# Nineteen differences per head for queries and keys: product halves of 304 columns instead of 320

## The chip, the cores and the metric

The kernel runs on one core of one Trainium2 chip. The metric is the device time of one launch in microseconds (us). A core has TensorE (PE, matrix products, with a queue of weight loads of its own, PEld), VectorE (DVE), ScalarE (ACT), GpSimd (POOL) and SyncE (SP), which here issues the DMA transfers. They run side by side and wait for one another through semaphores.

## The reference

There are 2048 rows of 640 values, 32 heads of 20 values, and two layers, each an attention step and a dense step (weights are the same in both layers):

```python
def _A_ref(x, wqkv, w_phi, wo):
    qkv = (x @ wqkv).reshape(B, S, 3, H, Dh) ...
    q, k, v = qkv[0], qkv[1], qkv[2]
    pq = einsum("bhsd,hdf->bhsf", q, w_phi)
    pk = einsum("bhsd,hdf->bhsf", k, w_phi)
    phi_q = concatenate([softmax(pq), softmax(-pq)], axis=-1)
    phi_k = concatenate([softmax(pk), softmax(-pk)], axis=-1)
    kv = einsum("bhsf,bhsd->bhfd", phi_k, v)
    z  = einsum("bhsf->bhf", phi_k)
    num = einsum("bhqf,bhfd->bhqd", phi_q, kv)
    den = einsum("bhqf,bhf->bhq", phi_q, z)[..., None] + 1e-6
    return (num / den) ... @ wo
def _B_ref(x, w1, b1, w2):
    h = x @ w1 + b1
    return (h * tanh(softplus(h))) @ w2
x = x + _A_ref(_layernorm(x), ...)
x = x + _B_ref(_layernorm(x), ...)
x = x + _A_ref(_layernorm(x), ...)
x = x + _B_ref(_layernorm(x), ...)
```

A softmax over the 20 values of a head does not change when the same number is subtracted from all of them. That holds for `pq`, `-pq`, `pk` and `-pk`.

## The kernel before

**Tiles.** The rows are worked on in 8 blocks of 256, each of two tiles of 128 rows. Every product is taken in three parts: a 32-bit value is split into a high part (`hi`, rounded to the format `fp32r`) and the rest (`lo`), and hi x hi, hi x lo and lo x hi are added up in PSUM. The inner dimension of 640 is 5 pieces of 128. One projection of a tile (`project`) is therefore two halves of 320 columns (`HC`), each 15 matmuls (`project_half`, L344), and a half fits one bank of PSUM.

**The first half of attention** (`attend_first`). For each tile there are a projection for keys, for queries and for values. `w_phi` has been folded into the query and key weights once, at the start of layer 0: `fold_phi` multiplies raw weights with a block-diagonal matrix of six heads (`bd`, L237) and splits the product into hi (ACT, L242) and lo (DVE, L243). The folded weights are written to `wp_d` in DRAM (`spill_qk_weights`) and fetched again for layer 1. Then `features` makes both softmaxes of a tile: ACT copies the 640 products from PSUM into every second group of 20 of the tile `e` (the `act` at L361; the profile shows ordered ACT instructions under L116, the line of the helper), DVE takes maximum and minimum per head (L368), subtracts (L371; L369 on DVE for keys, on POOL for queries), ACT takes the exponential of all 1280 values, DVE adds up each group and takes reciprocals (L377, L378), and POOL multiplies (L379). Keys then go into the sum with the values on PE (L414, 22 matmuls a tile). Queries are transposed in 32x32 pieces by DVE (L423) and written to DRAM (`e_d`), to be read again turned. The transposed, normalised rows of a block come in hi and lo (`Transposed.step`; the lo is L286 on DVE, tile `xtl`).

**The second half** (`attend_second`) multiplies the query features with the sums (L571), divides, projects with `wo` (again L344) and adds to the rows. **The dense layer** multiplies in L679 (256 columns) and L721 (320 columns), with the activation in between.

**Order.** The first half and the dense layer are under `tc.block(schedule_with_timeline_sim=True)`: a planner arranges the instructions of each engine by estimated durations. `attend_second` has PE and SP in the order in which it is written, and so has SP at the start. ACT instructions made with `act` are kept in program order relative to one another. `pending` and `advance` push the steps of older tiles on while a newer one is projected. The order of tiles in a block is a list:

```python
order = ("k0", "v0", "q0", "k1", "v1", "q1")
if b == 0:
    order = ("v0", "q0", "v1", "k0", "q1", "k1")
elif b == 1:
    order = ("k0", "q0", "k1", "v0", "q1", "v1")
elif b == NB - 1:
    order = ("k0", "k1", "v0", "v1", "q0")
```

Two PSUM tiles of two banks (`mm`) and four of one (`one`) are shared by all products.

Of the kernel before, what the change touches and what calls it, by code (L numbers as in the profile page):

```python
# [8 lines left out]
F32 = mybir.dt.float32  # L9
F32R = mybir.dt.float32r  # L10
AF = mybir.ActivationFunctionType
ALU = mybir.AluOpType
# [4 lines left out]
P = 128  # L17
S = 2048
D = 640
F = 1536  # L20
H = 32
# [6 lines left out]
NT = S // P  # L28
G = 11
HC = D // 2  # L30
EW = 2 * D
GW = 3 * (DH + 1)
GP = 6
# [9 lines left out]
def kernel(  # L43
# [131 lines left out]
    def load_q_weights():  # L175
        ws = [r2_pair(k) for k in range(KD)]
        for k in range(KD):
            for s in range(2):
                nc.sync.dma_start(ws[k][s].bitcast(F32), wp_d[0, s, k])
        return ws  # L180

    def load_k_weights(kv_ws):
        for k in range(KD):
            for s in range(2):
                nc.sync.dma_start(kv_ws[k][s][:, :D].bitcast(F32), wp_d[1, s, k])
# [26 lines left out]
    def load_raw(which, ts=range(6)):  # L212
# [11 lines left out]
            raw.append((r, rows))  # L224
        return raw

    def fold_phi(ws, bd, raw):

        pss = {}
        for k, c in ((0, 0), (1, 0), (2, 0), (3, 0), (0, 1), (1, 1), (2, 1), (3, 1), (4, 0), (4, 1)):  # L230
            if c == 0:
                mm = None if k % 2 else mm_tile()
                pss[k] = [one_tile(), one_tile()] if k % 2 else [mm[:, 0], mm[:, 1]]
            ps = pss[k][c]
            for t in range(3 * c, 3 * c + 3):
                r, rows = raw[t]
                nc.tensor.matmul(ps[:, (t % 3) * 120:(t % 3) * 120 + rows],  # L237
                                 r[:rows, k * P:(k + 1) * P], bd[:rows, t, :rows],
                                 start=True, stop=True)
# [86 lines left out]
        return Transposed(cols=cols)  # L326


    def project(xts, t, ws, col, ps=None):

        if ps is None:
            mm = mm_tile()
            ps = [mm[:, 0], mm[:, 1], mm]
        for c in range(2):
            project_half(ps[c], xts, t, ws, col, c)
        return ps

    def project_half(ps, xts, t, ws, col, c, ks=range(KD)):
        sl = slice(t * P, (t + 1) * P)
        cs = slice(col + c * HC, col + (c + 1) * HC)  # L340
        for k in ks:
            h, l, wh, wl = xts.hs[k], xts.ls[k], ws[k][0][:, cs], ws[k][1][:, cs]
            for n, (a, r) in enumerate(((h, wh), (h, wl), (l, wh))):
                nc.tensor.matmul(ps[:, :HC], a[:, sl], r, start=(k == 0 and n == 0),  # L344
                                 stop=(k == KD - 1 and n == 2))

    def both(ps):

        return ps[2][:, :, :HC]


    def query_tile(i):
# [2 lines left out]
    def features(ps, e, pool_sub):  # L355

        eg = e.rearrange("p (g d) -> p g d", d=DH)
        eh = e.rearrange("p (h s d) -> p s h d", s=2, d=DH)
        ec = e.rearrange("p (c h s d) -> p s c h d", c=2, s=2, d=DH)[:, 1]
        if len(ps) > 2:  # L360
            act(ec, both(ps).rearrange("p c (h d) -> p c h d", d=DH), AF.Copy)  # L361
        else:
            for c in range(2):
                act(ec[:, c], ps[c][:, :HC].rearrange("p (h d) -> p h d", d=DH), AF.Copy)
        yield
        m = work.tile([P, 2, H], F32, tag="m", name="m", bufs=2)
        for s, op in ((0, ALU.max), (1, ALU.min)):
# [19 lines left out]
    def attend_first(layer, x_src, first):  # L387
# [57 lines left out]
        if first is None:  # L445
            with tc.manual_schedule(engines={mybir.EngineType.SP}):
                bd = big_tile()[:120, :720].rearrange("p (t c) -> p t c", t=6)
                nc.sync.dma_start(bd[:, :3], phi_bd[:, :3])
                raw = load_raw(0, range(3))
                xt = fetch_normed(0)  # L450
                nc.sync.dma_start(bd[:, 3:], phi_bd[:, 3:])
# [49 lines left out]
        def rest():  # L501

            ps = [one_tile(), one_tile()]
            project_half(ps[0], xts, 1, q_ws, 0, 0)
            advance()
            advance()
            yield
            project_half(ps[1], xts, 1, q_ws, 0, 1, range(3))
            yield
            project_half(ps[1], xts, 1, q_ws, 0, 1, range(3, KD))  # L510
# [369 lines left out]
```

## Time and profile before

| | us |
|---|---|
| median of 3 runs | 1411.07 |
| lowest and highest | 1410.63 and 1412.09 |
| span of the profiled execution | 1410.6 |
| PE, PEld busy | 1391.5, 1369.5 |
| DVE, ACT, POOL busy | 1077.9, 583.6, 460.6 |

The profiled execution's own time is its span of 1410.6 us, from its first to its last instruction; the median of the runs is 0.5 us more. Busy shares are averages over stages. The first half of attention takes about 20 to 270 us in layer 0 and 718 to 968 us in layer 1, the dense layers follow the second halves. A matmul's busy time overlaps with the next one's, so the distance between starts is what a matmul costs. In groups by line, the columns are line, engine, operation, output<-input, shapes and count, then busy us and mean ns of one, then the idle time of the engine just before them with what ended it. In a timeline, the columns are start, duration, engine, line, operation, output<-input, shapes, count, and in brackets the idle time before. Rows of windows give, after the window, the busy time and count of each engine, the granted clock of PE, the DMA share and GB/s.

### The profile page before, as it was taken

To read this page: it belongs to the slowest core of one execution; us is meant where nothing else is said; L and a number is where in the kernel's file an instruction comes from. 1 tells how busy PE (TensorE), PEld (TensorE's weight loads), DVE (VectorE), ACT (ScalarE), POOL (GpSimd) and SP (SyncE) were. 2 spreads that over 40 slices of the span, in tenths; PEclk is the share of its full clock that TensorE was granted. 3 is DMA by queue.
4 is the path that set the end of the run, shared out by engine and by line. 5 is a ranking of instruction groups with operands and counts; after the bars stand their busy time and mean duration, and the time that the engine had idled before them with its cause. 6 is when DMAs were issued, how large, how long until landed. Compare 5 with 4: busy or idle time off the path is not lost. (4 is left out here: it accounts for less than half of the span.)

```text
span 1410.6 us, 28124 instructions
## 1 busy us (share of the span) xinstructions
PE 1391.5 (99%) x11528; PEld 1369.5 (97%) x11528; DVE 1077.9 (76%) x1810; ACT 583.6 (41%) x973; POOL 460.6 (33%) x344
## 2 busy tenths in 40 slices
PE   7999999999999999999999999999999999999998
PEld 7999999999999999999999999999999999999998
DVE  4798877686688877788769887878767766767765
ACT  4444343321355554455454333332234444444443
POOL 1354444343442221222234443443434211111112
PEclk9999999999999999999999999999999999999999
DMA  8533422789633423343374333357966212333200
GB/s 315 169 78 57 75 38 39 198 231 298 220 100 94 101 77 63 98 113 94 105 270 87 73 65 67 49 113 225 293 229 206 56 31 83 94 94 94 65 30 20
DMA packets 350035, 169.57 MB, mean 120 GB/s; under 512 B 286866, under 2 KB 323458, under 8 KB 349906
## 3 DMA queue, kind: packets, MB, share of 16 engines
q1 hardware_dynamic: 349906, 167.78, 44.1%
q8 instruction: 90, 1.47, 0.4%
q14 instruction: 39, 0.32, 0.1%
HBM read 104.82 MB, written 62.91 MB: 119 GB/s over the span
## 5 line engine op out<-in xcount | busy, mean ns | idle before, releaser
L721 PE MATMUL mm<-r2h,ol 128*128 128x320 f32 x1280 | 305.5, 310 | 1.4 <-ACT ol L704 0.8
L705 POOL TENSOR_TENSOR ol<-big,ol 128x512 fp32r<-128x512 f32 (+1 forms) x98 | 130.0, 1327 | 457.4 <-ACT ol L704 386.8
L679 PE MATMUL one<-xtl,r1h 128*128 128x256 f32 x960 | 268.6, 280 | 2.0 <-DVE xtl L286 2.0
L679 PE MATMUL one<-xth,r1l 128*128 128x256 f32 x960 | 268.0, 279 | 0.0
L679 PE MATMUL one<-xth,r1h 128*128 128x256 f32 x960 | 266.5, 279 | 0.0
L721 PEld LDWEIGHTS mm<-r2h,ol 128*128 128x128 f32 x1280 | 219.1, 188 | 3.1 <-POOL ol L705 1.8
L721 PE MATMUL mm<-r2l,ol 128*128 128x320 f32 x640 | 197.3, 309 | 0.0
L344 PE MATMUL mm<-r1h,xth 128*128 128x320 f32 x600 | 188.3, 314 | 0.0
L344 PE MATMUL mm<-r1h,xtl 128*128 128x320 f32 x600 | 185.7, 310 | 0.7 <-DVE xtl L286 0.7
L344 PE MATMUL mm<-r1l,xth 128*128 128x320 f32 x600 | 185.6, 309 | 0.0
L679 PEld LDWEIGHTS one<-xtl,r1h 128*128 128x128 f32 x960 | 180.4, 188 | 2.7 <-DVE xtl L286 2.5
L679 PEld LDWEIGHTS one<-xth,r1l 128*128 128x128 f32 x960 | 180.4, 188 | 0.0
L679 PEld LDWEIGHTS one<-xth,r1h 128*128 128x128 f32 x960 | 179.9, 188 | 0.0
L344 PE MATMUL mm<-r2h,xth 128*128 128x320 f32 x460 | 144.4, 314 | 0.0
L694 DVE TENSOR_SCALAR big<-big 128x512 f32<-128x512 f32 (+1 forms) x98 | 55.8, 570 | 113.4 <-ACT big L692 111.3
L344 PE MATMUL mm<-r2h,xtl 128*128 128x320 f32 x460 | 142.4, 310 | 0.0
L344 PE MATMUL mm<-r2l,xth 128*128 128x320 f32 x460 | 142.3, 309 | 0.0
L379 POOL TENSOR_TENSOR r<-r,r 128x1280 f32<-128x1280 f32 x32 | 75.7, 2367 | 144.5 <-DVE r L378 138.9
L692 ACT ACTIVATE big<-one,b1s 128x256 f32<-128x256 f32 x192 | 80.8, 469 | 96.0 <-PE one L679 93.8
L721 PEld LDWEIGHTS mm<-r2l,ol 128*128 128x128 f32 x640 | 120.2, 188 | 0.0
L696 ACT ACTIVATE big<-big,two 128x512 f32<-128x512 f32 (+1 forms) x98 | 70.1, 715 | 118.7 <-DVE big L695 116.2
L704 ACT ACTIVATE ol<-big 128x512 fp32r<-128x512 f32 (+1 forms) x98 | 61.0, 622 | 133.6 <-DVE big L703 133.3
(128 smaller groups left out, 3088.2 us busy)
## 6 DMA issues: line engine op xcount, KB each, us to landing
e_d<-r SPq DMA_DIRECT2D x128, 160.0 KB, 4.0
big<-e_d SPq DMA_DIRECT2D x32, 640.0 KB, 7.2
x_d<-xt SPq DMA_DIRECT2D x23, 640.0 KB, 4.1
xt<-x_d SPq DMA_DIRECT2D x22, 640.0 KB, 5.4
n_d<-xn SPq DMA_DIRECT2D x176, 80.0 KB, 2.1
xt<-in_x SPq DMA_DIRECT2D x16, 640.0 KB, 6.7
xn<-x_d SPq DMA_DIRECT2D x28, 320.0 KB, 4.3
v<-n_d SPq DMA_DIRECT2D x30, 256.0 KB, 3.1
```

The lines of the kernel that those rows point to most:

```text
L344: nc.tensor.matmul(ps[:, :HC], a[:, sl], r, start=(k == 0 and n == 0), stop=(k == KD - 1 and n == 2))
L379: nc.gpsimd.tensor_tensor(eg, eg, r.unsqueeze(2).to_broadcast([P, 2 * H, DH]), op=ALU.mult)
L679: nc.tensor.matmul(ph[:, j, :], l, r, start=(n == 0), stop=(n == 3 * KD - 1))
L692: exps[0] = nc.scalar.activation(part(ta, 0)[:, j - js.start], ph[:, j, :], AF.Exp, bias=b1s[:, 2 * pr + j:2 * pr + j + 1]).ins
L694: nc.vector.tensor_scalar_min(e, e, E_CAP)
L696: nc.scalar.activation(r, n, AF.Ln, bias=two)
L704: nc.scalar.activation(ah[:, js], n, AF.Copy)
L705: nc.gpsimd.tensor_tensor(al[:, js], n, ah[:, js].bitcast(F32), op=ALU.subtract)
L721: nc.tensor.matmul(pys[t][:, c, :HC], l[:, j, sl], r, start=(f == 0 and n == 0), stop=(f == KF - 1 and n == 2))
```

## The change

Per head, the first of the 20 product columns is subtracted from the other 19 in the block-diagonal matrix, before it is folded into the weights. So the folded weights of queries and keys have 19 columns a head, 608 in all, and the two halves of a projection have 304 columns. The twentieth value of a head, the first in its place, is the constant zero, written into the tile `e` by an additional ACT instruction. Everything from the maximum on works on 20 values as before. Values and output projection keep halves of 320.

```diff
+DF = DH - 1
+FC = H * DF // 2
+FW = H * DF
...
-    wp_d = dram.tile([2, 2, KD, P, D], F32, name="wp_d")
+    wp_d = dram.tile([2, 2, KD, P, FW], F32, name="wp_d")
...
-                nc.sync.dma_start(wp_d[1, s, k], kv_ws[k][s][:, :D].bitcast(F32))
-                nc.sync.dma_start(wp_d[0, s, k], q_ws[k][s].bitcast(F32))
+                nc.sync.dma_start(wp_d[1, s, k], kv_ws[k][s][:, :FW].bitcast(F32))
+                nc.sync.dma_start(wp_d[0, s, k], q_ws[k][s][:, :FW].bitcast(F32))
...
+    def differences(bd, ts):
+
+        part = bd[:, ts].rearrange("p t (h d) -> p (t h) d", d=DH)
+        nc.vector.tensor_tensor(part[:, :, 1:], part[:, :, 1:],
+                                part[:, :, :1].to_broadcast([120, 18, DF]), op=ALU.subtract)
...
-                nc.tensor.matmul(ps[:, (t % 3) * 120:(t % 3) * 120 + rows],
-                                 r[:rows, k * P:(k + 1) * P], bd[:rows, t, :rows],
+                n, c0 = rows // DH, (t % 3) * 6 * DF
+                nc.tensor.matmul(ps[:, c0:c0 + n * DF].rearrange("p (h d) -> p h d", d=DF),
+                                 r[:rows, k * P:(k + 1) * P],
+                                 bd[:rows, t].rearrange("p (h d) -> p h d", d=DH)[:, :n, 1:],
                                  start=True, stop=True)
-            n0, n1 = (0, 360) if c == 0 else (360, D)
+            n0, n1 = (0, 18 * DF) if c == 0 else (18 * DF, FW)
...
-    def project_half(ps, xts, t, ws, col, c, ks=range(KD)):
+    def project_half(ps, xts, t, ws, col, c, ks=range(KD), w=HC):
         sl = slice(t * P, (t + 1) * P)
-        cs = slice(col + c * HC, col + (c + 1) * HC)
+        cs = slice(col + c * w, col + (c + 1) * w)
...
-                nc.tensor.matmul(ps[:, :HC], a[:, sl], r, start=(k == 0 and n == 0),
+                nc.tensor.matmul(ps[:, :w], a[:, sl], r, start=(k == 0 and n == 0),
...
+        act(eh[:, 1, :, 0], ident[:, :H], AF.Copy, scale=0.0)
         if len(ps) > 2:
-            act(ec, both(ps).rearrange("p c (h d) -> p c h d", d=DH), AF.Copy)
+            act(ec[..., 1:], both(ps, FC).rearrange("p c (h d) -> p c h d", d=DF), AF.Copy)
         else:
             for c in range(2):
-                act(ec[:, c], ps[c][:, :HC].rearrange("p (h d) -> p h d", d=DH), AF.Copy)
+                act(ec[:, c, :, 1:], ps[c][:, :FC].rearrange("p (h d) -> p h d", d=DF), AF.Copy)
...
-            yield from features(project(xts, i % BT, kv_ws, 0), e, False)
+            yield from features(project(xts, i % BT, kv_ws, 0, w=FC), e, False)
...
-            yield from features(project(xts, i % BT, q_ws, 0) if ps is None else ps, e, True)
+            yield from features(project(xts, i % BT, q_ws, 0, w=FC) if ps is None else ps, e, True)
...
                 bd = big_tile()[:120, :720].rearrange("p (t c) -> p t c", t=6)
                 nc.sync.dma_start(bd[:, :3], phi_bd[:, :3])
                 raw = load_raw(0, range(3))
+                differences(bd, slice(0, 3))
                 xt = fetch_normed(0)
                 nc.sync.dma_start(bd[:, 3:], phi_bd[:, 3:])
                 raw += load_raw(0, range(3, 6))
+                differences(bd, slice(3, 6))
```

The loads of the weights in layer 1 and the four calls in `rest`, which projects the last query tile of each layer, change in the same way.

More of the change, by code (lines that the diff above doesn't have):

```diff
@@ L178, in load_q_weights @@
             for s in range(2):
-                nc.sync.dma_start(ws[k][s].bitcast(F32), wp_d[0, s, k])
+                nc.sync.dma_start(ws[k][s][:, :FW].bitcast(F32), wp_d[0, s, k])
         return ws
@@ L184, in load_k_weights @@
             for s in range(2):
-                nc.sync.dma_start(kv_ws[k][s][:, :D].bitcast(F32), wp_d[1, s, k])
+                nc.sync.dma_start(kv_ws[k][s][:, :FW].bitcast(F32), wp_d[1, s, k])
     def spill_qk_weights(kv_ws, q_ws):
@@ L326, in load_turned, with project @@
         return Transposed(cols=cols)
-    def project(xts, t, ws, col, ps=None):
+    def project(xts, t, ws, col, ps=None, w=HC):
         if ps is None:
@@ L343, in project_half, with both @@
             for n, (a, r) in enumerate(((h, wh), (h, wl), (l, wh))):
-                nc.tensor.matmul(ps[:, :HC], a[:, sl], r, start=(k == 0 and n == 0),
+                nc.tensor.matmul(ps[:, :w], a[:, sl], r, start=(k == 0 and n == 0),
                                  stop=(k == KD - 1 and n == 2))
-    def both(ps):
-        return ps[2][:, :, :HC]
+    def both(ps, w=HC):
+        return ps[2][:, :, :w]
     def query_tile(i):
@@ L503, in rest @@
             ps = [one_tile(), one_tile()]
-            project_half(ps[0], xts, 1, q_ws, 0, 0)
+            project_half(ps[0], xts, 1, q_ws, 0, 0, w=FC)
             advance()
@@ L507, in rest @@
             yield
-            project_half(ps[1], xts, 1, q_ws, 0, 1, range(3))
+            project_half(ps[1], xts, 1, q_ws, 0, 1, range(3), w=FC)
             yield
-            project_half(ps[1], xts, 1, q_ws, 0, 1, range(3, KD))
+            project_half(ps[1], xts, 1, q_ws, 0, 1, range(3, KD), w=FC)
             pending.append(queries(xts, NT - 1, ps))
```

2 lines of the change are left out of this document (1 added, 1 removed).

## The prediction

> **What bounds the kernel now.** The page comes first, for the engines' shares; then the waits of TensorE (PE), to see whether its busy time hides stalls; then the stages, since a share over the whole span mixes them. The lines of the page:
>
> ```profile
> span 1410.6 us, 28124 instructions
> PE 1391.5 (99%) x11528; PEld 1369.5 (97%) x11528; DVE 1077.9 (76%) x1810; ACT 583.6 (41%) x973; POOL 460.6 (33%) x344
> PEclk9999999999999999999999999999999999999999
> ```
>
> PE is busy 99% of the span at the full granted clock. What PE's waits show (us in total, times, longest):
>
> ```profile
> PE mm L237 <- DMA raw<-in_wqk_t: 8.3, 3, 4.2
> PE one L679 <- DVE xtl L286: 2.0, 2, 1.0
> PE one L414 <- POOL big L379: 0.9, 1, 0.9
> PE mm L344 <- DVE xtl L286: 0.7, 1, 0.7
> ```
>
> Over half of all waiting is the first 12 us, where weights have not landed. The attention's first half (queries, keys, values) is where the change acts; its windows give busy time per engine, PE, PEld (weight loads), DVE, ACT, POOL in turn:
>
> ```profile
> 60.00:101.00 41.00, 41.00 (x332) 39.77 (x331) 41.00 (x49) 19.14 (x27) 23.56 (x14) 1.00 0.39 71
> 101.00:245.00 144.00, 144.00 (x1102) 141.18 (x1102) 116.13 (x153) 57.44 (x81) 62.62 (x38) 1.00 0.34 57
> 735.00:792.00 57.00, 55.38 (x426) 54.03 (x425) 56.22 (x58) 24.34 (x38) 25.68 (x13) 1.00 0.41 80
> 792.00:945.00 153.00, 153.00 (x1163) 149.98 (x1162) 124.73 (x143) 54.67 (x78) 63.91 (x31) 1.00 0.39 71
> ```
>
> In the long steady stretches PE never stops and VectorE (DVE) fills 81% (116.13/144.00 and 124.73/153.00 are 0.81 and 0.82). At the start of each layer DVE is full as well (41.00 of 41.00; 56.22 of 57.00). So PE time saved in the steady part should come out of the total; near each layer's start, DVE may hold part of it.
>
> **The matmuls.** Busy time overlaps from one matmul to the next, so the price is the distance between starts. In the timeline, from one projection matmul to the 45th after it:
>
> ```profile
> 831.00 0.31 PE L344 MATMUL mm<-r1h,xth 128*128 128x320 f32 x1
> ...
> 837.60 0.31 PE L344 MATMUL mm<-r2h,xth 128*128 128x320 f32 x1
> ```
>
> 6.60 us / 45 = 146.7 ns for 320 columns. Whether fewer columns are faster is read from the dense layers, which have matmuls of 320 (L721) and 256 columns (L679) with the same 128x128 weight load; from the chain that ended last, and from the weight-load groups:
>
> ```profile
> 1131.95 3.50 PE one L679 x30
> 1135.45 3.53 PE mm L721 x24
> ...
> L679 PEld LDWEIGHTS one<-xth,r1l 128*128 128x128 f32 x960 | 180.4, 188 | 0.0
> L344 PEld LDWEIGHTS mm<-r1l,xth 128*128 128x128 f32 x600 | 112.8, 188 | 0.0
> ```
>
> 3.53/24 = 147.1 ns and 3.50/30 = 116.7 ns: 30.4 ns for 64 columns, 0.475 ns per column along this line, or 0.459 in plain proportion (147.1/320). The loads take 188 ns in both cases and are hidden in both, so the columns set the interval. 304 columns lie between the two measured sizes. 16 columns less are 7.34 to 7.6 ns; I take 7.35. The count is from the code: 16 tiles of rows, queries and keys, 2 halves x 15 matmuls, 2 layers: 16 x 2 x 30 x 2 = 1920. 1920 x 7.35 ns = **14.1 us saved** (bounds 14.1 to 14.6). Values and the output projection keep 320 columns.
>
> A rule stands beside that. The Trainium skill, "TensorE: Matmul & The Clock Gate", section Back-to-back issue gap, gives about N/2.4 + 2.5 ns for an isolated warm stream; by it 16 columns are 6.7 ns and the saving an estimated 12.8 us. The trace's 147 and 117 ns lie above that formula at both sizes, so the rows' slope is used.
>
> **The folded weights.** L237 multiplies 100 times with 120 columns and 20 times with 40; they become 114 and 38, read from a view of 19 of every 20. Six of them in a row:
>
> ```profile
> 36.34 0.82 PE L237 MATMUL mm<-big,raw 120*128 120x120 f32 x6
> 37.01 0.83 PE L237 MATMUL one<-big,raw 120*128 120x120 f32 x6
> ```
>
> (37.01 - 36.34)/6 = 112 ns, so 6 columns less are 5.6 ns, 0.56 us over 100. No row shows a read with gaps; I bound it by the same amount as a loss, and take 0.3 us saved, as part of them stand in stalls for their inputs. The evictions of the folded weights (342 and 266 columns, not 360 and 280) and the 40 transfers of them to and from DRAM shrink by 5%; no PE wait names them, so they count nothing.
>
> **The two subtractions.** They run on DVE over 120 x 342, and now the folds wait for them rather than for the transfer alone. The nearest rows in size:
>
> ```profile
> L584 DVE TENSOR_TENSOR xn<-mm,den 128x480 f32<-128x480 f32 x32 | 21.0, 657 | 1.0
> L584 DVE TENSOR_TENSOR xn<-mm,den 128x160 f32<-128x160 f32 x32 | 10.0, 313 | 0.0
> ```
>
> On that line 342 elements are 313 + 182 x 1.075 = 0.51 us. The first comes when the first block lands (4.2 us); PE's first four folds would start 0.5 later, still ahead of the 1.01 us pause for the next weights before 6.43, which takes it in. The second is less clear:
>
> ```profile
> big<-in_phi_bd SPq DMA_DIRECT2D x1, 168.8 KB, 7.5
> ...
> 3.05 0.44 SPq L451 DMA_DIRECT2D big<-in_phi_bd  x1
> ...
> 6.43 2.06 PE L237 MATMUL mm<-big,raw 120*128 120x120 f32 x8 [1.01 <-DMA raw<-in_wqk_t]
> 11.54 0.75 PE L237 MATMUL mm<-big,raw 120*128 120x120 f32 x2 [3.05 <-DMA raw<-in_wqk_t]
> ...
> 10.02 1.67 DVE L250 BATCH_NORM_STATS2 bn<-xt 128x6 f32<-128x320 f32 x4 [0.44 <-DMA xt<-in_x]
> 11.61 0.33 DVE L252 BATCH_NORM_AGGREGATE mv<-bn 128x2 f32<-128x12 f32 x2
> ```
>
> The second block lands at 3.05 + 7.5 = 10.55. Ahead of the statistics, the subtraction ends near 11.1 and PE does not notice, but the row statistics, the normalising and the transposes queued behind it on DVE come 0.5 later; behind them it ends near 11.94 + 0.51 = 12.45, and the folds, with ACT and DVE waiting for their results, start 0.9 later. Between 0 and 1.0 us I take **0.5 lost**.
>
> **The extra write and the copy.** 64 more ACT writes of 128x32, one ahead of each copy of products into the tile. The same kind of write exists for the values:
>
> ```profile
> L116 ACT ACTIVATE v<-ident 128x32 f32<-128x32 f32 x32 | 8.3, 261 | 0.0
> L116 ACT ACTIVATE big<-mm 128x640 f32<-128x640 f32 x32 | 22.6, 707 | 101.5 <-PE mm L344 101.5
> L116 ACT ACTIVATE r<-mm 128x640 f32<-128x640 f32 x30 | 21.2, 705 | 68.0 <-PE mm L344 58.8 <-DMA e_d<-r 9.2
> ```
>
> 64 x 0.261 = 16.7 us of ACT. But ACT sits idle 101.5/32 = 3.2 us and 68.0/30 = 2.3 us ahead of each copy, waiting for the products; the write needs only a free tile and goes there. The ordered list puts it right before the copy, which needs that same free tile (the 9.2 us on DMA), so nothing new is held up: 0 us. Without that cover every copy would be 0.26 late, 16.7 in all if PE felt each. The copy of 608 instead of 640 elements gains some 27 ns ((707 - 261)/608 x 32 = 23), off the path.
>
> **What DVE gives back.** DVE's work per tile is unchanged (the twentieth value is still reduced, exponentiated and scaled), so where DVE is full PE only arrives sooner. At the start of layer 1:
>
> ```profile
> 760.16 0.81 DVE L369 TENSOR_TENSOR big<-big,m 128x640 f32<-128x640 f32 x1
> ...
> 771.60 2.62 POOL L379 TENSOR_TENSOR big<-big,r 128x1280 f32<-128x1280 f32 x1 [5.84 <-DVE r L378]
> ...
> 771.92 2.98 DVE L369 TENSOR_TENSOR big<-big,m 128x640 f32<-128x640 f32 x1
> ...
> 775.97 2.84 DVE L286 TENSOR_TENSOR xtl<-xn,xth 128x512 fp32r<-128x512 f32 x1
> ...
> 781.58 1.04 DVE L286 TENSOR_TENSOR xtl<-xn,xth 128x256 fp32r<-128x256 f32 x1
> ...
> 782.67 0.42 PE L344 MATMUL mm<-r1h,xtl 128*128 128x320 f32 x1 [0.73 <-DVE xtl L286]
> ```
>
> Block 2's last transposed low half is ready only at 782.6. From 735, by the order of the code, 7 query and key tiles run before that: 7 x 30 x 7.35 ns = 1.5 us that PE saves and then waits for. In layer 0 the same piece is just in time:
>
> ```profile
> 91.12 0.36 DVE L286 TENSOR_TENSOR xtl<-one,xth 128x256 fp32r<-128x256 f32 x1
> ...
> 92.22 0.41 PE L344 MATMUL mm<-r1h,xtl 128*128 128x320 f32 x1
> ```
>
> Ready at 91.48, used at 92.22: 0.74 us to spare, against some 0.95 saved since 60 (4.3 query and key tiles of 30 matmuls in the order of the code): 0.2 lost. Together **1.7 lost**. Later, slack is ample; a key tile's last step on POOL against its use:
>
> ```profile
> 143.23 2.37 POOL L379 TENSOR_TENSOR big<-big,r 128x1280 f32<-128x1280 f32 x1 [5.29 <-DVE mv L252]
> ...
> 150.28 0.94 PE L414 MATMUL one<-big,v 128*64 128x120 f32 x14
> ```
>
> 145.6 to 150.28 is 4.7 us; a whole block gets only 120 x 7.35 ns = 0.88 us shorter.
>
> **Sum.** -14.1 - 0.3 + 0.5 + 1.7 = -12.2 us. On the profiled span, 1410.6 - 12.2 = 1398.4; the median of the runs is 1411.07, 0.5 above the span, so **1398.9 us**.
>
> **Rivals.** (1) DVE takes more. If DVE is what ends each block wherever it is full, and the order written anew by the planner from new durations costs a little besides, half the gain goes: 1411.1 - 7 = 1404, up to 1406. For it speak the full DVE windows; against it the 19% DVE slack over the 297 us of steady stretches. 10%.
>
> (2) The weight loads bound PE. PEld is busy 97% and every load stays, so nothing is gained: 1411.1 + 0.5 = 1411.6. Against it: the interval fell from 147 to 117 ns over loads of one length. 3%. The Trainium skill, "Perfetto Trace Analysis", section Identifying the Most-Contended Engine, takes the share of weight-load time as the measure of how near PE is to its limit, and would have these 97% as the bound; the two intervals disagree.
>
> (3) Slower: DVE and POOL collide. The L369 step of 2.98 us above ran beside POOL's multiplication (L379, 2.62 us); the same step at 760.16 took 0.81. That is 2.1 to 2.2 us for each collision; I take 2.1. A steady block has 24 of 29.4 us of DVE work (0.81 x 29.4, a block being 180 matmuls of 146.7 ns and 3 us of small ones). Shortened to 28.5 with a new order, it becomes DVE-bound from 28.5 - 24 = 4.5 us, two more collisions per block, and slower than before from 5.4. Three per block give 24 + 6.3 = 30.3, 0.9 us over 29.4; in the 10 steady blocks (297/29.4) that is 9 us: 1420. Against it: the order keeps its structure, and few collisions occur in the steady windows. 7%.
>
> (4) The new column count runs at the rate of the folds, 112/120 = 0.93 ns per column: 304 would be 284 ns, 137 more, 263 us in all, 1674. It decides as soon as an interval passes 146.7 ns. Nothing speaks for it but that no row has 304. 2%.
>
> **Numbers.** The forecast has 78%. Its own terms reach from -14.6 - 0.6 (1395.9; an order that happens to drop one of the small waits, 1394.5) to -14.1 + 0.6 + 1.0 + 4 (1402.6). Rival 1 extends the range to 1406; rivals 2, 3 and 4 stay outside, 12%. A difference under 0.2%, 2.8 us, is about what a measurement of this kernel cannot tell from none. Faster: 78 + 10 = 88%; same: 3%; slower: 7 + 2 = 9%.
>
> **What would show it.** Right: L344 groups of 1920 matmuls with 128x304, starts 139 to 140 ns apart; 64 writes of 128x32 near 0.26 us, with no PE wait on ACT; a steady block of 28.5 us; a longer wait on xtl (L286 before) near 780, 2 us rather than 0.7; the folds (L237) starting within 1 us of before. Wrong: intervals still at 147 ns (rival 2) or above (rival 4), DVE without idle time in the steady windows (rivals 1 and 3), or PE waits summing to over 20 us.

## The result and the profile after

The two kernels were run in turn on one chip, five times each. Before took 1412.09 us (median; 1410.63 to 1414.52), after 1405.88 us (1405.29 to 1406.86): the ratio is 0.9955, with a 95% interval from 0.9942 to 0.9967. That is 6.2 us faster, half of the 12.2 forecast. The profiled spans say the same: 1410.6 and 1404.1, 6.5 us apart. (The forecast started from 1411.07 for before, 1.0 below the median measured here, so it is the difference that is compared.) The page of the kernel after:

```profile
span 1404.1 us, 28174 instructions
PE 1381.4 (98%) x11528; PEld 1359.2 (97%) x11528; DVE 1077.1 (77%) x1812; ACT 591.1 (42%) x1037; POOL 466.4 (33%) x344
```

PE is 10.1 us less busy than before (1391.5), but the span shrank by 6.5 only. So PE waits more, which its waits show (us in total, times, longest):

```profile
PE mm L247 <- DMA raw<-in_wqk_t: 5.0, 2, 4.2
PE mm L355 <- ACT r L119: 5.0, 2, 2.7
PE mm L247 <- DVE big L233: 3.3, 1, 3.3
PE one L693 <- DVE xtl L297: 2.0, 2, 1.0
```

The folds (L247, before L237) wait 8.3 us in all, as before; 3.3 of them now go by the second subtraction. New is the second row: 5.0 us in two waits for a copy from PSUM by ACT (L119). Gone are the 0.9 us on POOL and the 0.7 us on `xtl` that the attention's first half had. The windows say where the new waits are (after each window: busy time of PE, PEld, DVE, ACT, POOL; granted clock, DMA share, GB/s):

```profile
60.00:101.00 41.00, 38.67 (x297) 37.33 (x297) 40.16 (x47) 16.33 (x26) 22.33 (x13) 0.96 0.40 74
101.00:245.00 144.00, 144.00 (x1142) 141.09 (x1141) 118.77 (x156) 61.42 (x102) 66.69 (x38) 1.00 0.33 56
735.00:792.00 57.00, 54.26 (x417) 52.68 (x416) 55.27 (x58) 23.02 (x42) 25.21 (x13) 0.97 0.43 84
792.00:945.00 153.00, 153.00 (x1192) 150.11 (x1191) 126.97 (x144) 59.83 (x102) 66.99 (x32) 1.00 0.41 76
```

In the two long stretches PE never stops and gets through 40 and 29 more instructions than before. In the two short ones at the start of each layer it does fewer (297 and 417, before 332 and 426), and its granted clock, 1.00 before, is 0.96 and 0.97. The steady price of the new matmul is read from the timeline (start, duration, engine, line, operation), 20 starts in a row, of which the first and the last:

```profile
103.26 0.30 PE L355 MATMUL mm<-r2h,xth 128*128 128x304 f32 x1
...
105.92 0.30 PE L355 MATMUL mm<-r2l,xth 128*128 128x304 f32 x1
```

2.66 us / 19 = 140.0 ns, where 320 columns take 146.7. The groups by line give the prices of the added instructions and of the shorter copies (busy us, mean ns, then the idle time before):

```profile
L233 DVE TENSOR_TENSOR big<-big 120x342 f32<-120x342 f32 x2 | 1.0, 510 | 2.4 <-DMA big<-in_phi_bd 2.4
L119 ACT ACTIVATE r<-ident 128x32 f32<-128x32 f32 x32 | 8.3, 260 | 28.6 <-DMA e_d<-r 19.8 <-DVE r L390 8.7
L119 ACT ACTIVATE r<-mm 128x608 f32<-128x608 f32 x30 | 20.3, 677 | 40.9 <-PE mm L355 40.9
```

The write of a query tile (`r<-ident`) now takes over the wait for the tile that the copy (`r<-mm`) had: ACT is idle 28.6 us ahead of it, and for 28.5 of these something still to finish with the tile is named. Before, 9.2 us stood there.

**The stall in layer 0.** PE's timeline around 89 us, after:

```profile
86.59 0.31 PE L355 MATMUL mm<-r1h,xtl 128*128 128x320 f32 x1
89.23 0.41 PE L355 MATMUL mm<-r1h,xth 128*128 128x304 f32 x1 [2.33 <-ACT r L119]
...
89.91 0.46 PE L355 MATMUL mm<-r1h,xth 128*128 128x304 f32 x1
...
92.44 0.46 PE L355 MATMUL mm<-r1l,xth 128*128 128x304 f32 x1
...
94.18 0.41 PE L355 MATMUL mm<-r1h,xth 128*128 128x320 f32 x1
```

PE could have gone on at 86.74 (one interval after 86.59) and starts at 89.23. From 89.91 to 92.44 ten intervals take 2.53 us, 253 ns each and not 140: the granted clock is 0.50 there (its rows stand in the last section). What PE waited for is on ACT, first after, then before:

```profile
88.38 0.26 ACT L119 ACTIVATE r<-ident 128x32 f32<-128x32 f32 x1 [9.56 <-DMA e_d<-r]
88.51 0.66 ACT L119 ACTIVATE r<-mm 128x608 f32<-128x608 f32 x1
```

```profile
85.31 0.70 ACT L116 ACTIVATE r<-mm 128x640 f32<-128x640 f32 x1 [3.26 <-DMA e_d<-r]
```

A query tile is one of two buffers. The copy of query tile 3 needs the buffer of query tile 1, and that is free when its four transfers to `e_d` have landed. Until then the products stay in PSUM, and as there are two PSUM tiles (`mm`), PE stands still when it needs a third. Before, the same copy waited for the same transfer, but PE came for the PSUM tile late enough:

```profile
88.77 0.31 PE L344 MATMUL mm<-r1h,xth 128*128 128x320 f32 x1
```

The copy was done at 86.01 and the tile was used at 88.77: 2.8 us to spare. After, it is done at 89.17 (3.2 later) and wanted at 86.74 (2.0 earlier): 5.2 - 2.8 = 2.4 us of stall. (0.6 us of the 2.0 is only this profile's earlier start, 18.54 and not 19.10 for its first projection; counted from there, PE is 1.5 us earlier and the copy 3.7 later, the same 5.2.) PE is earlier as intended; why the copy is later is on DVE and SP. The rows of after, then those of before (DVE turns the tile, SP then issues its transfers):

```profile
74.03 2.98 DVE L383 TENSOR_TENSOR r<-m,r 128x640 f32<-128x640 f32 x1
...
77.40 1.60 DVE L261 BATCH_NORM_STATS2 bn<-xt 128x6 f32<-128x320 f32 x4
78.93 1.52 DVE L380 TENSOR_REDUCE m<-big 128x32 f32<-128x640 f32 x2
80.37 1.50 DVE L435 STREAM_TRANSPOSE r<-r 128x1280 f32<-128x1280 f32 x1
```

```profile
81.90 3.27 SPq L439 DMA_DIRECT2D e_d<-r  x4
```

```profile
77.33 1.50 DVE L423 STREAM_TRANSPOSE r<-r 128x1280 f32<-128x1280 f32 x1
...
79.45 0.81 DVE L371 TENSOR_TENSOR r<-m,r 128x640 f32<-128x640 f32 x1
```

```profile
78.85 3.29 SPq L427 DMA_DIRECT2D e_d<-r  x4
```

The planner, whose order follows estimated durations, now puts three steps ahead of the turning that stood behind it: the row statistics of the next block (L261, before from 84.37), the second of a key tile's two reductions (L380; before, one stood ahead at 76.60 and one behind at 78.75), and the subtraction that DVE does for the next query tile (L383). The last took 0.81 us in its old place; in the new one it runs beside a multiplication on POOL (L391, 73.39 to 76.34) and takes 2.98. Other steps moved too, so the transfers are issued 3.05 us later and not by the sum of the three.

**The stall in layer 1** has the same form. PE's rows, then DVE's, of after:

```profile
757.25 1.38 PE L426 MATMUL one<-big,v 128*64 128x120 f32 x22
761.29 0.41 PE L355 MATMUL mm<-r1h,xth 128*128 128x320 f32 x1 [2.66 <-ACT r L119]
...
762.24 0.47 PE L355 MATMUL mm<-r1h,xtl 128*128 128x320 f32 x1
...
764.91 0.47 PE L355 MATMUL mm<-r1h,xth 128*128 128x320 f32 x1
```

```profile
746.29 2.98 DVE L383 TENSOR_TENSOR r<-m,r 128x640 f32<-128x640 f32 x1
...
752.78 1.50 DVE L435 STREAM_TRANSPOSE r<-r 128x1280 f32<-128x1280 f32 x1
```

Ten intervals from 762.24 take 2.67 us, 267 ns each, half speed again. The turning is that of the layer's first query tile. It comes 38.3 us after the layer's first projection (714.5); before it came at 749.00, 31.3 us after 717.7. Here too a query tile's subtraction has come to stand ahead of it and takes 2.98 us. (The write's idle time in this layer is put down to the reciprocals, L390, but these had ended at 754.7. Still under way were the tile's four transfers, issued between 754.30 and 757.5, which take 2.5 to 4.0 us to land.)

**The balance.** 1920 x 6.7 ns = 12.9 us are saved. Two stalls (2.4 + 2.7) and the halved clock behind them (1.5 + 1.5, measured below) take 8.1; the waits that vanished (0.9 + 0.7) give 1.6 back: 12.9 - 8.1 + 1.6 = 6.4, against 6.5 between the spans.

### The profile page after: what moved, and what is told of

It is laid out like the page before. It is cut to its first block, busy times and chain, and to the rows that moved or that the text cites. A ratio compares the mean times of both kernels' runs of the same rounds, so it can differ in the third digit from the quotient of the medians.

```text
span 1404.1 us, 28174 instructions
## 1 busy us (share of the span) xinstructions
PE 1381.4 (98%) x11528; PEld 1359.2 (97%) x11528; DVE 1077.1 (77%) x1812; ACT 591.1 (42%) x1037; POOL 466.4 (33%) x344
## 4 chain that ended last, share of the span: by engine, by line
PE 87%; DVE 7%; DMA 2%; ACT 1%; issue 1%; SPq 0%; POOL 0%; DVEq 0%; ACTq 0%; POOLq 0%
PE mm L355 28%; PE one L693 22%; PE mm L735 21%; PE one L355 7%; PE mm L585 3%; PE one L426 3%; PE one L291 2%; DVE m L380 1%; DVE big L708 1%; DVE r L389 1%; PE mm L247 1%; DVE xtl L297 1%; DVE big L715 1%; DMA v<-in_wv 1%; DVE big L709 0%
## 5 line engine op out<-in xcount | busy, mean ns | idle before, releaser
L355 PE MATMUL mm<-r1h,xth 128*128 128x304 f32 (+1 forms) x600 | 187.8, 313 | 5.0 <-ACT r L119 5.0
L355 PE MATMUL mm<-r1l,xth 128*128 128x304 f32 (+1 forms) x600 | 185.0, 308 | 0.0
L355 PE MATMUL mm<-r1h,xtl 128*128 128x304 f32 (+1 forms) x600 | 184.8, 308 | 0.1
L355 PE MATMUL mm<-r2h,xth 128*128 128x304 f32 (+1 forms) x460 | 142.2, 309 | 0.0
L355 PE MATMUL mm<-r2h,xtl 128*128 128x304 f32 (+1 forms) x460 | 140.4, 305 | 0.0
L355 PE MATMUL mm<-r2l,xth 128*128 128x304 f32 (+1 forms) x460 | 140.3, 305 | 0.0
L391 POOL TENSOR_TENSOR r<-r,r 128x1280 f32<-128x1280 f32 x32 | 76.9, 2404 | 138.1 <-DVE r L390 131.9
L355 PEld LDWEIGHTS mm<-r1h,xth 128*128 128x128 f32 x600 | 114.0, 190 | 7.3 <-ACT r L119 5.4
```

Source lines behind the costliest of these rows:

```text
L355: nc.tensor.matmul(ps[:, :w], a[:, sl], r, start=(k == 0 and n == 0), stop=(k == KD - 1 and n == 2))
L391: nc.gpsimd.tensor_tensor(eg, eg, r.unsqueeze(2).to_broadcast([P, 2 * H, DH]), op=ALU.mult)
```

## The experiments

Against the reading above (the query tile comes free late by the order, and PE needs its PSUM tile early) stood two rivals: that the added write on ACT costs this by itself, and that DVE has too much to do at the start of a layer, so that a stall taken away there comes back elsewhere. The intervals of the ratios reach some 1.2 to 2.1 us to either side, so differences of 1 to 3 us between the variants rest on their profiles more than on their times. The table gives, from each profile, the start of the first matmul of the dense layer in layer 0, the same counted from the first projection (which starts between 18.2 and 19.1 us in these profiles), and the time from layer 1's first projection to the end.

| kernel | dense layer 0 from | from the first projection | layer 1 to end | span |
|---|---|---|---|---|
| before | 378.8 | 359.7 | 692.9 | 1410.6 |
| after | 375.6 | 357.1 | 689.6 | 1404.1 |
| third tile | 372.4 | 353.7 | 689.7 | 1400.9 |
| third tile in layer 0 alone | 372.9 | 354.1 | 688.9 | 1400.6 |
| the same, turning first in layer 1 | 371.7 | 353.6 | 688.2 | 1398.8 |
| the same, subtractions on POOL | 372.6 | 353.9 | 686.8 | 1398.3 |

**A third query tile, after and before.** Query tiles 2 and 3 go to a buffer of another kind, so that the copy no longer waits for `e_d`. Both kernels got the same edit:

```diff
     def query_tile(i):
+        if i in (2, 3):
+            return big_tile()
         return r2_wide(10 + i % 2, F32)...
```

> The changed kernel, with query tiles 2 and 3 of each layer in a tile of the big pool instead of the two query tiles, so their copies need not wait until tiles 0 and 1 have been turned and read out. Theory A (the query copy waits for its tile, the products stay in PSUM, TensorE stalls 2.3 and 2.7 us and then runs some 3 us at half clock, twice 1.2 us): both waits of TensorE on the query copy go, the clock stays at 1.00 near 90 and 760 us, and the time falls by 4 to 7.6 us, to 1398 to 1402. Rival B (the 64 extra ScalarE writes cost the time): no change, 1406, as they stay. Rival C (VectorE is the bound at the start of each layer and the lost part cannot be had): 1404 to 1406, with the waits turned into others on VectorE.

> The kernel before with the same two query tiles moved to the big pool. Theory A: TensorE did not wait for a query copy there, so the time stays within 0.2% (1409 to 1414). Rival C: the same. A gain of 4 us or more would mean that the tile is worth it whatever the width of the products.

On after: 1403.19 us, ratio 0.9941 (0.9929 to 0.9953), above the 1398 to 1402 that theory A gave. On before: 1411.07, 0.9996 (0.9987 to 1.0005), nothing. So the wait for the buffer costs nothing before and stalls PE only with the change. Layer 0 now gains 6.4 us over before (6.1 from the first projection on), about the whole of its share of 12.9. Layer 1 gains nothing by it: the waits moved. Windows and waits of after with the third tile:

```profile
60.00:101.00 41.00, 40.77 (x334) 39.18 (x333) 38.93 (x49) 18.82 (x30) 25.43 (x15) 1.00 0.41 75
735.00:792.00 57.00, 53.70 (x415) 52.08 (x414) 50.96 (x55) 22.04 (x37) 25.37 (x12) 0.97 0.38 74
```

```profile
PE one L428 <- POOL big L393: 2.3, 2, 1.2
PE mm L355 <- ACT xth L119: 1.0, 1, 1.0
```

In the first window the clock is back at 1.00 and PE at 334 instructions (before 332). In layer 1 there are now 3.3 us of waits on key tiles and transposed rows (at 765, 773 and 776), and the clock is still 0.97.

The edit changed more than the buffers. DVE's order in layer 0 changed with it: the turning of query tile 1 comes 59.3 us after the first projection (58.2 before, 61.8 after), and none of DVE's eleven subtractions of 128x640 in the first window takes over 1.5 us, where three of ten do in after. So this run doesn't tell the buffer from the order.

**The write alone**, in the kernel before (it writes a value that the copy then overwrites):

```diff
+        act(eh[:, 1, :, 0], ident[:, :H], AF.Copy, scale=0.0)
         if len(ps) > 2:
             act(ec, both(ps)..., AF.Copy)
```

> The kernel before with the 64 extra ScalarE writes alone (the copy of 640 values writes over them). Theory A: the write waits for nothing that the copy does not wait for, so within 0.2% (1409 to 1414), unless the planner orders VectorE otherwise, which would show as a TensorE wait on the query copy. Rival B: slower by about what is missing in the changed kernel, 5 to 7 us, 1417 to 1419.

1413.71 us, ratio 1.0017 (1.0008 to 1.0025): 2.4 us slower than before, not the 6 missing and not nothing. PE's waits grew on `xtl`, and on POOL from 0.9 to 1.2, by a new order on DVE; no wait on ACT appeared:

```profile
PE mm L344 <- DVE xtl L286: 2.1, 2, 1.4
```

**The write on DVE** in place of ACT, in after:

```diff
-        act(eh[:, 1, :, 0], ident[:, :H], AF.Copy, scale=0.0)
 ...
         yield
+        nc.vector.memset(eh[:, 1, :, 0], 0.0)
         m = work.tile([P, 2, H], F32, tag="m", name="m", bufs=2)
```

> The changed kernel with the zero written by VectorE just ahead of the maximum instead of by ScalarE ahead of the copy: 64 small VectorE writes of some 0.06 us, 4 us of VectorE work in all. Theory A: the copy itself still waits for the tile, so the stalls stay and the time is 1405 to 1408. Rival B: the lost part comes back, 1399 to 1401. Rival C: slightly slower than the change, by up to 1 us per layer's start, 1406 to 1408.

1407.33 us, ratio 0.9969 (0.9959 to 0.998), not faster than after. The two layers have to be read apart. In layer 1 the wait for the query copy is there without any write by ACT, 2.46 of these 3.1 us at the same place, so there the write is not its cause:

```profile
PE mm L355 <- ACT r L119: 3.1, 2, 2.5
```

In layer 0 the stall is gone, with the two old query buffers and with more work on DVE (a write takes 0.09 us, not the 0.06 expected). The window, and the turning in it:

```profile
60.00:101.00 41.00, 41.00 (x339) 39.79 (x338) 40.42 (x55) 19.35 (x27) 23.37 (x14) 1.00 0.41 75
```

```profile
78.71 1.50 DVE L435 STREAM_TRANSPOSE r<-r 128x1280 f32<-128x1280 f32 x1
```

That is 58.9 us after the first projection (58.2 before, 61.8 after). The row statistics and both reductions still stand ahead of the turning. The query tile's subtraction doesn't: it comes at 82.29 and takes 0.77 us. So in layer 0 moving the write from ACT to DVE does end the stall, by way of DVE's order, and of the three steps that had moved it is the subtraction beside POOL that went back. What hides the gain in the time are above all two new waits of PE of 1.81 us, one in each second half, for the rows (`xt`, L615); just ahead of these rows DVE does a subtraction that takes 2.53 us beside POOL. This profile also starts 1.3 us later than after.

**The turning first, in layer 0.** Row statistics and reductions that stood ahead of it are issued behind it:

```diff
+            if after in turned:
+                with tc.issue_after(turned[after]):
+                    nc.vector.tensor_reduce(m[:, s], eh[:, 1], axis=AX.X, op=op)
 ...
-                        xt = fetch_normed(b + 1)
+                        xt = fetch(x_src, b + 1) if late else fetch_normed(b + 1)
 ...
+                            with tc.issue_after(turned[0, 1]):
+                                norm_scale(b + 1, [norm_stats(t_, xt) for t_ in range(BT)])
```

> The changed kernel, layer 0 only: VectorE's statistics of block 2 and the two reductions of key tile 3, which its order has ahead of the turning of query tile 1, are queued behind it. Theory A1 (the change made the planner put 3.1 us of other VectorE work ahead of the turning, so the tile comes free too late): the turning starts near 77.4 us instead of 80.4, TensorE's wait of 2.3 us near 89 us and the half clock behind it go, and layer 0 ends 2.5 to 3.5 us earlier: 1402.5 to 1403.5. Rival A2 (TensorE is simply early and VectorE is full, so any order gives the same): the wait comes back under another name (xtl, L426) and the time stays within 1 us of 1405.9.

1414.45 us, ratio 1.0017 (1.0008 to 1.0026). The turning came at 76.42, 4 us earlier, and its stall went, but the edit moved the normalising too. In ACT's timeline:

```profile
87.33 1.73 ACT L119 ACTIVATE xn<-xt,stats 128x640 f32<-128x640 f32 x2 [12.83 <-DVE stats L273]
```

ACT's ordered instructions all stood 12.83 us behind this one, and PE waited 7.0 us for `xn`. The run says nothing on the question; it only shows what a late statistic costs. So the edit was made again without it.

**Only the two reductions behind the turning, in layer 0**: the first part of the diff above alone.

> The changed kernel with one thing in layer 0 queued otherwise: the maximum and minimum of key tile 3 on VectorE (1.5 us) behind the turning of query tile 1, not ahead of it. Theory A1 (VectorE's order ahead of the turning keeps the query tile too long): turning at about 78.9 us instead of 80.4, TensorE's wait near 89 us 0.8 instead of 2.3 us, layer 0 ends 1.5 us earlier or, if the shorter gap leaves the clock alone, 3 us: 1403 to 1404.5. Rival A2 (VectorE is full, any order costs the same): another wait takes its place, 1405 to 1407.

1404.57 us, ratio 0.9945 (0.9932 to 0.9959), 1.3 us less than after, with intervals that overlap. This profile starts 0.9 us later (first projection at 19.40), and the turning of query tile 0 comes 1.2 later; against these, the turning of tile 1 (80.07) is 1.2 to 1.5 us earlier. PE's wait in layer 0:

```profile
88.91 0.41 PE L355 MATMUL mm<-r1h,xth 128*128 128x304 f32 x1 [0.89 <-ACT r L119]
```

1.5 us less on DVE's queue, 1.4 us less stall (2.33 in after), and no halved clock behind it: the next starts are 0.14 apart. So moving two instructions in DVE's order is enough to take most of this stall away. A wait of 0.9 us on `xth` took the place of some of it.

**Filling the stalls.** 16 matmuls of 320 columns, whose product nobody reads, stand at each of the two places where PE waits:

```diff
+                if (layer, b, n) in ((0, 2, 0), (1, 1, 3)):
+                    fill = one_tile()
+                    for f in range(16):
+                        nc.tensor.matmul(fill[:, :HC], xts.hs[0][:, :P], q_ws[0][0][:, :HC],
+                                         start=True, stop=True)
```

> The changed kernel with 16 added matmuls of 320 columns (2.35 us, no use of the result) at each of the two places where TensorE waits for the query copy: ahead of key tile 4 in layer 0 and of value tile 2 in layer 1. They should fit into the waits. Theory D (an idle gap of over 2 us makes the clock go to half for some 3 us, 1.2 us each): the clock stays at 1.00 in both stretches and the time falls by about 2.4 us, to 1403.5, though work was added. If the slow matmuls after the gap have another cause: 1405.9 or, where the added work isn't hidden, up to 1410.6.

1405.75 us, ratio 0.9955 (0.9943 to 0.9968): as fast as after, though PE does 2 x 2.35 us more. The clock is 1.00 in both short windows, and the same 14 matmuls and 22 small ones after the stall take less time:

```profile
89.75 0.41 PE L355 MATMUL mm<-r1h,xth 128*128 128x304 f32 x1
...
93.22 0.41 PE L355 MATMUL mm<-r1h,xtl 128*128 128x304 f32 x1
```

3.47 us, where after has 94.18 - 89.23 = 4.95: 1.5 us for the halved clock. In layer 1 the same stretch takes 4.51 and not 6.04 us, again 1.5. The price of the lower clock is shown; the total, which was to fall by both, is a miss. Up to the dense layer the profile gains 1.0 us (374.6 against 375.6), or 1.5 counted from the first projection (355.6 against 357.1); layer 1 gave its part back (689.8 against 689.6), with waits of 0.8 us on `xtl`, 0.7 on POOL and 0.5 on the copy.

**A third tile in layer 0 alone** (`if layer == 0 and i in (2, 3)`):

> As the run with query tiles 2 and 3 in the big pool, but in layer 0 alone; layer 1 as in the changed kernel. Theory A: layer 0 gives its whole 6.4 us and layer 1 3.3 as in the changed kernel, 9.7 in all: 1401.5 to 1403.5, no better than both layers, since in layer 1 the other buffers only exchanged one wait for others. If layer 1 had gained by the tile: 1405.

1403.43 us, ratio 0.9939 (0.9926 to 0.9951), the same as with both. In layer 1 PE has its wait on the query copy (2.9 us) and the clock of 0.97 as in after. So the 2.5 us or so that a third tile gives come from layer 0.

**Less work for DVE at the start of layer 1.** On top of that, the subtraction of the maximum goes to POOL for key tiles 0 to 3 of layer 1; the same on before:

```diff
-            yield from features(project(xts, i % BT, kv_ws, 0, w=FC), e, False)
+            yield from features(project(xts, i % BT, kv_ws, 0, w=FC), e, layer == 1 and i < 4)
```

> As the run with query tiles 2 and 3 of layer 0 in the big pool, and in layer 1 the subtraction of the maximum of key tiles 0 to 3 on GpSimd instead of VectorE (four times 0.8 to 3.0 us less on VectorE, 1.3 us each more on GpSimd). Theory E (at the start of layer 1 the amount of VectorE's work is what holds TensorE): the waits near 760 and 780 us shrink, layer 1 gives 5 to 6.4 us instead of 3.3 to 4.0, 1400 to 1402. Rival (what counts is the order and the tiles that are kept, not the amount): 1403 to 1405.

> The kernel before with the same four subtractions of layer 1 on GpSimd. TensorE waited only 1.6 us there near 780 us, so at most that is gained: 1409.5 to 1412. A gain of 3 us or more would mean that the move is worth it without the change.

With the change: 1400.24 us (1399.46 to 1400.87), ratio 0.9914 (0.9901 to 0.9928), 11.8 us faster than before and the lowest time of this study. On before: 1410.37, ratio 0.9988 (0.9979 to 0.9997). The move is worth 1.7 us without the change and 3.2 by the times with it (2.1 by the profiles, from layer 1's start to the end). Against before with the same move, the change is worth 10.1 us here, not 11.8. The last window with the change:

```profile
735.00:792.00 57.00, 55.82 (x436) 53.98 (x436) 51.19 (x56) 23.59 (x40) 30.89 (x17) 1.00 0.45 85
```

The clock is whole, PE does 436 instructions (417 after), and its wait on the copy is 0.9 us. But the edit did several things: DVE has less to do (51.19 us, not 55.27), the planner's order brought the turning back to 31.6 us after the layer's start, and the two subtractions of 2.98 and 2.99 us beside POOL that after has at the start of layer 1 are gone (the longest now takes 1.93). In the eight other kernels with 304 columns told of so far or below (all but the next) it comes at 37.0 to 38.3, in the four with 320 at 31.2 to 32.0.

**The order alone, in layer 1.** To part order from amount: the third tile in layer 0, DVE's work unchanged, and the reductions of key tile 1 behind the turning.

```diff
+            yield from features(project(xts, i % BT, kv_ws, 0, w=FC), e, False,
+                                (1, 0) if layer == 1 and i == 1 else None)
```

> The kernel with the third query tile in layer 0 (1403.43 us, ratio 0.9939), and in layer 1 the two reductions of key tile 1 are issued behind the turning of query tile 0 on VectorE; nothing is left out and the amount of VectorE work is the same. The order planned for VectorE then has two steps of 1.53 and 0.81 us behind the turning that stood ahead of it (the reductions and the subtraction that follows them). Order theory (layer 1 loses because the turning, and with it the transfer that frees the query tile, comes late in the queue): the turning comes 2.3 us earlier (34.9 to 35.1 us after the layer's first projection, not 37.3), the wait of TensorE on the query copy falls from 2.9 to 0.4 to 0.7 us, the granted clock between 735 and 792 us goes from 0.97 to 0.99 or 1.00, and the time falls by 2.0 to 3.7 us: 1399.7 to 1401.5, ratio 0.9912 to 0.9925. Amount theory (VectorE has too much to do at the start of layer 1, whatever the order): the wait moves to another place, a key tile's last multiplication or the transposed low half, with the same 2 to 3 us in all: 1402.6 to 1404.2, ratio 0.9933 to 0.9945.

1401.30 us, ratio 0.993 (0.9916 to 0.9944). The turning comes 35.4 us after the layer's start, the wait on the copy falls to 0.9, and the clock in the window is 1.00, all as the theory of the order said. But PE now waits three times for `xtl`:

```profile
PE mm L355 <- DVE xtl L297: 2.3, 3, 1.4
PE mm L355 <- ACT r L119: 0.9, 1, 0.9
```

2.0 us of stall went and 2.1 us came (0.2 before the edit); from layer 1's start to the end it is 688.2 us, 0.7 less than without the edit. The time lies in the range of the one theory, the ratio between the two. So the order moves PE's waits, and with them the fall of the clock. That the sum of the waits is set by how much DVE has to do there fits (less work gained 2.1 us in the layer, the same work in another order 0.7), but it is not shown: the run with less work had another order too, and in this one a subtraction of 2.98 us beside POOL still stands ahead of the turning, at 741.74.

**The price of a column.** In after, the two halves of the values (not of queries and keys) become 240 and 400 columns:

```diff
-                pv = project(xts, i % BT, kv_ws, D)
+                pv = mm_tile()
+                for c, (h0, n) in enumerate(((0, 12), (12, 20))):
+                    project_half(pv[:, c], xts, i % BT, kv_ws, D, c, w=n * DH, c0=h0 * DH)
```

> The changed kernel with the products of the values (from tile 2 on) in 240 and 400 columns instead of twice 320; two copies instead of one. Measures the interval between starts at other widths of the same operands. If it is a constant and columns (N/2.4 + 13.4 ns, through 140.0 at 304 and 146.7 at 320): 113.4 and 180.1 ns. If it is in proportion (0.4597 ns per column): 110.3 and 183.9 ns. On the line through 256 and 320 columns of the dense layers (0.475): 109 and 185 ns. Time within 2 us of the changed kernel.

```profile
126.11 0.27 PE L356 MATMUL mm<-r1h,xth 128*128 128x240 f32 x1
...
127.68 0.27 PE L356 MATMUL mm<-r1h,xtl 128*128 128x240 f32 x1
127.79 0.35 PE L356 MATMUL mm<-r1h,xth 128*128 128x400 f32 x1
...
130.35 0.34 PE L356 MATMUL mm<-r1h,xtl 128*128 128x400 f32 x1
```

1.57/14 = 112 ns and 2.56/14 = 183 ns; the kernel took 1407.03 us, ratio 0.9963 (0.9949 to 0.9978). With 140.0 and 146.7 the steps are 0.44 ns per column from 240 to 304, 0.42 to 320 and 0.45 to 400. Neither plain proportion from 320 (110 and 183) nor a constant with 1/2.4 ns per column (113 and 180) fits both ends.

## Why the prediction was right and wrong

- **Matmuls, -14.1: right in kind, 1.2 us too large.** 1920 matmuls of 304 columns came, 140.0 ns apart, at the edge of the 139 to 140 forecast. The saving is 6.7 ns each, 12.9 us, below the bounds of 14.1 to 14.6. The slope taken, 0.459 ns per column, was plain proportion, the lower of its two; from 304 to 320 columns it is 0.42. Why it is smaller is open. The 6.7 ns are what the Trainium skill, "TensorE: Matmul & The Clock Gate", section Back-to-back issue gap, gives for 16 columns by its formula for isolated matmuls, a rule that the prediction weighed and put aside. Its slope of 1/2.4 agrees here with the step from 304 to 320; the whole interval (146.7 ns against 135.8 by its formula) and the steps to 240 and 400 do not.
- **Folded weights and subtractions, +0.2 net: right within what can be seen.** A subtraction takes 510 ns, as worked out. The folds wait 3.35 us at 11.59 rather than 3.05 at 11.54, and the waits of the start-up sum to 8.3 us in both.
- **The extra write and the copy, 0 us: the step that failed.** The write's price was right (260 ns), and so was where it stands. Wrong was "so nothing new is held up": PE was held up for 2.4 and 2.7 us by the copy behind the write, and 1.5 us more each time by the lower clock, 8.1 us in all. The prediction quoted 9.2 us in which ACT waits for `e_d` ahead of a query copy and took them for idle time. During them the copy holds a PSUM tile, and that had 2.8 us to spare. PE 2.0 us earlier and the turning 3.1 us later used them up. Slack was worked out for `xtl` and for the key tiles, not for this third way. The write alone is not the cause: on before it costs 2.4 us and PE waits for no copy, and without it on ACT the wait stays in layer 1. In layer 0 it went with the write, since DVE's order went back with it.
- **DVE gives back 1.7 near 782: hidden in this run, there once the stall is gone.** The wait on `xtl` did not grow to 2 us; it vanished, since PE stalled before it, and layer 1 lost 3.2 us of its share of 6.45, not the 1.5 forecast for it. With the turning moved forward, 2.3 us of waits on `xtl` came and the layer lost 1.8: near that sum, though 0.9 us of PE's waits there are still for the copy.
- **Not in the sum at all:** that a stall can halve the clock afterwards (2 x 1.5 us), and that new durations make the planner arrange DVE anew. Rival 1 named the order only as "a little besides".
- **The rivals.** The time is that of rival 1 (1404 to 1406): half the gain lost where DVE is full. Its cause, DVE where it is full, holds in part: in layer 0 the gain came back with the same work on DVE (third tile) and with more (the write on DVE), so there the amount of its work was not it; in layer 1 the waits came back on DVE's results. Rival 2 fell (weight loads are at 97% still and the interval shrank), and so did rival 4. Rival 3 fell for the steady stretch, where DVE fills 118.77 of 144 us, 82%; but the collision that it priced at 2.1 us stands ahead of both late turnings.

In layer 0 an earlier PE alone (2.0 us) would have stayed within the 2.8 us of slack, and a later copy alone (3.2) would have passed it by 0.4; it takes both for 2.4. That is worked out, not shown by a run. What makes the planner choose the later place stays open.

## What to carry to other kernels

Before counting a saving on the bounding engine, list every buffer it will come back to sooner, and work out for each when its holder lets go, also where the holder is an engine that "waits anyway". A change of durations is a change of order where a planner arranges the queues, so look for the steps whose end frees something (here a turning with its transfers) and see whether they moved. When a gain is lost in two places, mend them one at a time, and make each mend on the kernel before as well: a third tile gave back layer 0, less work on the second-busiest engine most of layer 1, and 10.1 of the 12.9 us were there once the 1.7 that the second mend gives without the change are taken off.

## What the runs showed of the hardware

A wait of 2.3 us was enough to halve PE's granted clock. Two windows of after, each 3.41 us long (the clock is the number after POOL's busy time):

```profile
86.14:89.55 3.41, 1.08 (x8) 0.83 (x7) 3.41 (x4) 1.17 (x3) 2.24 (x1) 1.00 0.42 67
89.55:92.96 3.41, 3.41 (x16) 3.11 (x16) 3.41 (x7) 1.92 (x5) 2.72 (x2) 0.50 0.03 10
```

At half clock 304 columns took 253 ns and 320 took 267, 1.8 times as long. The clock does not change at the gap. In after it changes at 89.55, 92.97, 761.98 and 765.39 us: twice 3.41 us apart, and 672.43 us, 197 times 3.413, between the first and the third. The other traces show changes on such a grid too, with other starting points. Between the start-up and the end, all of them agree with this: what counts is how long PE stood still between two points of the grid. After 2.0 to 3.4 us of standing still the clock was 0.50 up to the next point at least: 2.33 and 2.66 us in after, and five more kernels have such a place. After up to 1.8 us it stayed at 1.00, with one exception: 1.80 us together with 22 small matmuls (layer 1 with both third tiles). A gap of 2.08 us (layer 0 of the kernel with 240 and 400 columns) lay across a point of the grid, 0.5 us before it and 1.6 behind, and the clock stayed whole. So whether a stall of some 2 us costs 1.5 us more is partly luck. The Trainium skill, "TensorE: Matmul & The Clock Gate", section HAM oscillation — how this bites in real kernels, warns of gaps over about 3.4 us. The half rate agrees with these traces; the length does not, shorter gaps sufficed.

The subtraction of a query tile on DVE took 2.98 us at 74.03 beside a multiplication of 2.95 us on POOL (from 73.39), 2.98 at 746.29 beside one of 2.53 (from 746.07), and 0.81 us at 738.27. This is the collision that the prediction priced, and it stands in DVE's queue ahead of both late turnings.
